# A dense-GELU layer's forward and backward: from the scheduler's order with packed tails to a fixed emission order with metered derivative work

## The chip, the cores and the metric

One core of a Trainium2 chip runs one program. The metric is the device time of one execution in microseconds (us). All times are medians of several executions unless one look is named. The experiments ran in three rounds, each on one chip; the kernel before took 320.8 to 321.4 us (medians) on all three, so runs of different rounds are compared directly. Unless a text says otherwise, runs are of the fast state (within 1.5% of the fastest run of the same kernel). "Span" is the time from the first to the last instruction of the one execution that was profiled; a run's time is 1.7 to 2.2 us above its span here.

Engine names in the profile: PE is TensorE's matmuls, PEld its weight loads, DVE is VectorE, ACT is ScalarE, POOL is GpSimd, SP issues most DMA. A trailing q (SPq, POOLq) is the engine's instruction queue.

## The reference

```python
# x: [1, 2048, 448], w1: [448, 1792], w2: [1792, 448], all bf16
h   = gelu_tanh(x @ w1 + b1)
out = h @ w2 + b2
# returned: out and the gradients of x, w1, b1, w2, b2 for a given grad_out
```

The gradient of x needs `gelu'(z)` with `z = x @ w1 + b1`. Both kernels compute it elementwise (E below), store it in place of z as `Z`, and use it in the backward: `gh = (Z + 1) * (grad_out @ w2^T)`.

## The kernel before

The program has four stages, each limited by TensorE at best:

1. Forward, 4 blocks of 512 rows x 7 pairs of 128 hidden columns = 28 steps. A step is a pair of z tiles (`pair_mms`) and the second product of the step before (`chain_step`).
2. grad_w2: 14 sums of 16 matmuls.
3. Backward: 28 steps like the forward's, with w2^T and w1^T.
4. grad_w1: 6 + 2 x 1 sums of the same kind.

The contraction of 448 is 3 x 128 + 64. The kernel before packs the 64-row tails of the two tiles of a pair into the two halves of the array:

```python
def pair_mms(pss, lhs, rhs, fts):
    for h, ft in enumerate(fts):                       # 3 full matmuls for each tile
        for n, kt in enumerate((0, 1, 3) if h == 0 else (0, 1, 2)):
            nc.tensor.matmul(pss[h], lhsT=lhs[:, kt, fc], rhs=rhs[:, kt, :], start=(n == 0), stop=False)
    for h, ft in enumerate(fts):                       # the two 64-row tails, side by side
        kt, ps_ = (2, slice(0, DL)) if h == 0 else (3, slice(DL, P))
        nc.tensor.matmul(pss[h], lhsT=lhs[ps_, kt, fc], rhs=rhs[ps_, kt, :], start=False, stop=True)
```

The derivative of one pair is three ScalarE and seven VectorE operations on 128x1024 tiles. The letters are used throughout:

```python
def emit_E(b, c):
    nc.scalar.activation(out=s, in_=zc, func=ACT.Square)             # ScalarE
    nc.vector.tensor_scalar(out=v, in0=s, ...)                       # u, first half
    nc.vector.tensor_tensor(out=v, in0=v, in1=zc, op=ALU.mult)       # u, second half
    nc.scalar.activation(out=v, in_=v, func=ACT.Tanh, scale=GELU_C)  # ScalarE
    nc.scalar.activation(out=n, in_=v, func=ACT.Square)              # ScalarE
    nc.vector.tensor_scalar(out=y, in0=s, ...)
    nc.vector.tensor_tensor(out=y, in0=y, in1=zc, op=ALU.mult)
    nc.vector.tensor_scalar(out=n, in0=n, scalar1=-1.0, scalar2=1.0, ...)
    nc.vector.tensor_tensor(out=y, in0=y, in1=n, op=ALU.mult)
    nc.vector.tensor_tensor(out=zc, in0=y, in1=v, op=ALU.add)        # Z is final
```

No order is laid down: a scheduler orders each engine's instructions, with the forward's matmuls and evictions marked as high priority. x block 0 is transposed on TensorE with an identity matrix, b1 too, and b1 is added in ScalarE's evictions (four of 128x512 a step: gelu and identity for two tiles).

## Time and profile before

| | before |
|---|---|
| time | 321.35 us (321.01 to 321.94, 3 runs; 321.19 with the fourth that came with the result) |
| span of the profiled run | 318.7 us |
| first useful matmul | 20.9 us |
| forward, 28 steps | 20.9 to 127.5 us, 3.8 us a step |
| grad_w2 | 127.5 to 170.1 us |
| start of the backward, with its stall | 170.1 to 183.7 us |
| backward at a steady step | 3.24 us a step |

The table of windows of the kernel before, cut near the stage borders (the second row ends with the first 1.7 us of the backward's matmuls, from 170.1). After the window and its length it gives busy us and, in brackets, instructions of each engine, then the granted TensorE clock, the DMA share and GB/s.

```profile
core 0: us, PE busy (x) PEld busy (x) DVE busy (x) ACT busy (x) POOL busy (x), PEclk, DMA share, GB/s
20.90:127.50 106.60, 101.23 (x448) 38.97 (x449) 56.03 (x107) 102.71 (x152) 5.93 (x5) 0.99 0.51 105
127.50:171.80 44.30, 44.30 (x235) 22.63 (x234) 43.47 (x86) 42.88 (x52) 7.04 (x8) 1.00 0.59 122
171.80:183.70 11.90, 4.39 (x18) 1.32 (x16) 11.83 (x27) 8.46 (x9) 0.71 (x1) 0.73 0.69 186
183.70:271.50 87.80, 87.77 (x425) 37.17 (x426) 37.34 (x115) 6.13 (x14) 2.29 (x3) 0.98 0.52 109
...
```

In the forward ScalarE is the full engine (102.7 of 106.6 us). In the third row VectorE is full (11.83 of 11.9) and TensorE does 4.4 us of work: the backward wants `Z`, and VectorE still owes derivatives. The clock of 0.73 there is the price of the pause: after the longest wait, of 4.8 us, four matmuls take 1.67 us (at 183.73), where four at 176.30 take 0.93.

The start, from the timeline of the kernel before (start, duration, engine, line, operation, and in brackets what the engine waited for):

```profile
12.87 0.28 POOL masks.py:199 TENSOR_SCALAR_AFFINE_SELECT ident<-ident 128x128 bf16<-128x128 bf16 x1 [10.27 <-issue]
12.99 0.64 DVE L220 TENSOR_TENSOR gsum<-g_all 128x448 f32<-128x448 bf16 x1 [11.86 <-DMA g_all<-in_grad_out_dram]
...
13.66 5.89 DVE L222 TENSOR_TENSOR gsum<-gsum,g_all 128x448 f32<-128x448 f32 x9
...
19.47 0.41 DVE L127 COPY xT_q<-acc 128x512 bf16<-128x512 bf16 x1
...
20.90 1.01 PE L71 MATMUL ps<-xT_q,w_sb 128*128 128x512 bf16 x2 [0.79 <-DVE b1c L132]
```

The scheduler hoisted the sums for grad_b2 (gsum) ahead of the copy of the transposed x, so VectorE first waited for g_all and then added for 6 us.

VectorE on derivative work, from the timeline of VectorE alone, kernel before:

```profile
143.32 0.42 DVE L152 TENSOR_SCALAR y<-s 128x1024 bf16<-128x1024 bf16 x1
143.65 0.42 DVE L154 TENSOR_SCALAR n<-n 128x1024 bf16<-128x1024 bf16 x1
143.99 0.68 DVE L149 TENSOR_TENSOR v<-v,Z_100 128x1024 bf16<-128x1024 bf16 x1
144.59 0.69 DVE L155 TENSOR_TENSOR y<-y,n 128x1024 bf16<-128x1024 bf16 x1
```

The starts are 0.33 to 0.34 us apart behind a TENSOR_SCALAR and 0.60 behind a TENSOR_TENSOR.

### The profile page before, as it was taken

To read this page: it belongs to the slowest core of one execution; us is meant where nothing else is said; L and a number is where in the kernel's file an instruction comes from. 1 tells how busy PE (TensorE), PEld (TensorE's weight loads), DVE (VectorE), ACT (ScalarE), POOL (GpSimd) and SP (SyncE) were. 2 spreads that over 40 slices of the span, in tenths; PEclk is the share of its full clock that TensorE was granted. 3 is DMA by queue.
4 is the path that set the end of the run, shared out by engine and by line. 5 is a ranking of instruction groups with operands and counts; after the bars stand their busy time and mean duration, and the time that the engine had idled before them with its cause. 6 is when DMAs were issued, how large, how long until landed. Compare 5 with 4: busy or idle time off the path is not lost.

```text
span 318.7 us, 3910 instructions
## 1 busy us (share of the span) xinstructions
PE 288.4 (91%) x1408; PEld 125.9 (40%) x1408; DVE 156.8 (49%) x348; ACT 171.5 (54%) x244; POOL 19.3 (6%) x26
## 2 busy tenths in 40 slices
PE   7238999999999997999997399999999999999994
PEld 2213343333333333555553034444444444555552
DVE  0380438267466558999999964343534343000000
ACT  1117999999999999999999600200200200312211
POOL 2003000100000000111002000000000000100000
PEclk9659999999999999999999679999999999999999
DMA  7993436735633556997004743665754554210111
GB/s 218 355 228 61 70 80 134 145 68 116 156 67 81 108 132 139 203 220 168 29 29 125 181 82 69 151 121 100 180 93 99 123 100 82 89 45 29 43 45 29
DMA packets 97998, 36.62 MB, mean 115 GB/s; under 512 B 90044, under 2 KB 95532, under 8 KB 97980
## 3 DMA queue, kind: packets, MB, share of 16 engines
q1 hardware_dynamic: 94924, 27.17, 41.3%
q0 software_dynamic: 2512, 8.95, 9.1%
q10 hardware_dynamic: 544, 0.26, 0.3%
q8 instruction: 11, 0.18, 0.2%
q14 instruction: 7, 0.06, 0.1%
HBM read 7.69 MB, written 6.89 MB: 46 GB/s over the span
## 4 chain that ended last, share of the span: by engine, by line
PE 63%; DVE 22%; ACT 9%; DMA 4%; issue 2%; DVEq 0%; POOL 0%; POOLq 0%; ACTq 0%
PE acc L138 23%; PE ps L71 20%; PE acc L276 11%; PE ps L75 6%; DMA g_all<-in_grad_out_dram 4%; DVE y L155 3%; DVE v L149 3%; DVE y L153 3%; ACT hT L180 3%; DVE v L148 2%; PE acc L284 2%; DVE gsum L222 2%; DVE n L154 2%; DVE y L152 2%; ACT Z_101 L181 1%
## 5 line engine op out<-in xcount | busy, mean ns | idle before, releaser
L138 PEld LDWEIGHTS <-hT 128*128 128x128 bf16 x448 | 38.7, 98 | 59.8 <-issue 14.1
L138 PE MATMUL acc<-w_sb,hT 128*128 128x448 bf16 x224 | 55.1, 354 | 3.5 <-ACT hT L180 2.4
L138 PE MATMUL acc<-w1T_sb,hT 128*128 128x448 bf16 x224 | 47.6, 358 | 7.5 <-DVE hT L242 7.5
L164 ACT ACTIVATE o_blk<-acc 128x448 bf16<-128x448 f32 x16 | 7.4, 550 | 82.3 <-issue 41.7
L71 PE MATMUL ps<-xT_q,w_sb 128*128 128x512 bf16 x168 | 45.9, 388 | 2.6 <-DVE b1c L132 0.8
L212 PE MATMUL acc<-g_all,h_nat 128*128 128x448 bf16 x224 | 42.5, 352 | 0.0
L71 PE MATMUL ps<-gT_q,w2T_sb 128*128 128x512 bf16 x168 | 42.2, 387 | 0.0
L180 ACT ACTIVATE hT<-ps,b1c 128x512 bf16<-128x512 f32 x56 | 38.5, 734 | 3.9 <-PE ps L75 3.7
L276 PE MATMUL acc<-gh_nat,x_all 128*128 128x448 bf16 x192 | 36.7, 352 | 0.0
L150 ACT ACTIVATE v<-v 128x1024 bf16<-128x1024 bf16 x28 | 30.0, 1086 | 3.2 <-DVE v L149 3.2
L151 ACT ACTIVATE n<-v 128x1024 bf16<-128x1024 bf16 x28 | 30.2, 1091 | 0.2
L212 PEld LDWEIGHTS <-h_nat 128*128 128x128 bf16 x224 | 21.9, 98 | 20.5
L71 PEld LDWEIGHTS <-w_sb 128*128 128x128 bf16 x168 | 16.4, 99 | 28.8 <-issue 13.7
L276 PEld LDWEIGHTS <-x_all 128*128 128x128 bf16 x192 | 18.6, 98 | 17.6 <-issue 0.4
L154 DVE TENSOR_SCALAR n<-n 128x1024 bf16<-128x1024 bf16 x28 | 11.8, 421 | 26.1 <-ACT n L151 26.1
L71 PEld LDWEIGHTS <-w2T_sb 128*128 128x128 bf16 x168 | 16.3, 99 | 18.9 <-issue 1.8
L278 ACT ACTIVATE gw_t<-acc 128x448 bf16<-128x448 f32 x12 | 6.5, 543 | 29.3 <-PE acc L276 27.3
L148 DVE TENSOR_SCALAR v<-s 128x1024 bf16<-128x1024 bf16 x28 | 11.9, 425 | 15.3 <-ACT s L147 14.3
L155 DVE TENSOR_TENSOR y<-y,n 128x1024 bf16<-128x1024 bf16 x28 | 19.2, 687 | 0.3
L75 PE MATMUL ps<-xT_q,w_sb 64*128 64x512 bf16 x56 | 17.5, 384 | 0.0
L165 POOL DMA_DIRECT2D out_dram<-o_blk x8 | 6.2, 770 | 172.2 <-DVE o_blk L162 99.1
L242 DVE SCALAR_TENSOR_TENSOR hT<-Z_99,ps 128x512 bf16<-128x512 bf16 x14 | 9.1, 686 | 13.5 <-PE ps L75 13.5
(69 smaller groups left out, 256.7 us busy)
## 6 DMA issues: line engine op xcount, KB each, us to landing
out_dram<-o_blk POOLq DMA_DIRECT2D x8, 448.0 KB, 4.0
g_all<-in_grad_out_dram POOLq DMA_DIRECT2D x1, 1792.0 KB, 11.7
x_all<-in_x_dram POOLq DMA_DIRECT2D x1, 1792.0 KB, 9.2
out_dram<-gw_t POOLq DMA_DIRECT2D x7, 224.0 KB, 3.0
out_dram<-gw_t SPq DMA_DIRECT2D x12, 112.0 KB, 1.7
w_sb<-in_w_dram SPq DMA_DIRECT2D x1, 1120.0 KB, 12.3
h_nat<-hT SPq DMA_TRANSPOSE x56, 2.4
gh_nat<-hT SPq DMA_TRANSPOSE x56, 2.5
```

Of the source, the lines that this page charges most:

```text
L71: nc.tensor.matmul(pss[h], lhsT=lhs[:, kt, fc], rhs=rhs[:, kt, :], start=(n == 0), stop=False)
L75: nc.tensor.matmul(pss[h], lhsT=lhs[ps_, kt, fc], rhs=rhs[ps_, kt, :], start=False, stop=True)
L138: nc.tensor.matmul(acc[j][:, 0:D], lhsT=lhs[:, h, j * P:(j + 1) * P], rhs=w[:, ft, :], start=(ft == 0), stop=(ft == NF - 1))
L148: nc.vector.tensor_scalar(out=v[:], in0=s[:], scalar1=GELU_A, scalar2=1.0, op0=ALU.mult, op1=ALU.add)
L149: nc.vector.tensor_tensor(out=v[:], in0=v[:], in1=zc, op=ALU.mult)
L150: nc.scalar.activation(out=v[:], in_=v[:], func=ACT.Tanh, scale=GELU_C)
L151: nc.scalar.activation(out=n[:], in_=v[:], func=ACT.Square)
L154: nc.vector.tensor_scalar(out=n[:], in0=n[:], scalar1=-1.0, scalar2=1.0, op0=ALU.mult, op1=ALU.add)
L155: nc.vector.tensor_tensor(out=y[:], in0=y[:], in1=n[:], op=ALU.mult)
L180: nc.scalar.activation(out=hT[:, h, :], in_=pss[h][:], func=ACT.Gelu_apprx_tanh, bias=b1c[:, ft:ft + 1])
L212: nc.tensor.matmul(ps_w[:, 0:D], lhsT=h_nat[:, st, ft * P:(ft + 1) * P], rhs=g_all[:, st, :], start=(st == 0), stop=(st == NS - 1))
L276: nc.tensor.matmul(ps_w[:, 0:CW], lhsT=x_all[:, st, kt * P:(kt + 1) * P], rhs=gh_nat[:, st, cs], start=(st == 0), stop=(st == NS - 1))
```

## The change: intent and diff

The intent is a plan in which TensorE never waits: one fixed order on all engines, the pipeline laid out by hand, and the derivative, which is off the critical path, dealt out in small portions ("metered") where an engine is thought to be idle. The diff, cut to its core:

```diff
+    ctx.enter_context(tc.manual_schedule())          # every engine in emission order
-    psum_z ... bufs=4 tiles of 128x512
+    psum_z ... bufs=2 tiles of 128x2x512             # one eviction of 128x1024 for a pair
+    class Background:                                # queues "V" (VectorE) and "A" (ScalarE)
+        def step(self, dve, act):                    # adds credits; emits queued operations
+            for e, c in (("V", dve), ("A", act)):    # while credit > 0 and their
+                self.credit[e] = min(self.credit[e] + c, 4.0)   # predecessor is emitted
+            ...
 # pair_mms: packed tails -> a fourth full matmul; rows 0..63 of its weights are zero,
 # but row 0 holds b1 and row 0 of xT holds ones
+            for kt in range(KD):
+                nc.tensor.matmul(ps[:, h, :], lhsT=lhs[:, kt, ...], rhs=rhs[:, kt, :], ...)
+    xq = load_x(0)                                   # x block 0 by DMA transpose, no identity
 # forward, step p
+            nc.scalar.activation(out=hT[:], in_=ps[:], func=ACT.Gelu_apprx_tanh)
+            nc.scalar.activation(out=Z[b][:, 2 * c:2 * c + 2, :], in_=ps[:], func=ACT.Identity)
+            if pc % 2 == 0:                          # 16 of 28 pairs now; uses hT, one Square less
+                emit_E(pb, pc, hist[p - 1], p - 1, prevs, False)
+            else:
+                late.append((pb, pc))                # 12 "late" pairs, in grad_w2
+        bg.step(dve, STEP - 2.16)                    # STEP = 3.24
 # zero rows of w2T for the padded backward
+    nc.gpsimd.memset(w2T_sb[0:DL, KD - 1, :], 0.0)
+    for k, (b, c) in enumerate(late):
+        emit_E(b, c, None, 100 + k, prevs, True)
+    for st in range(1, NS): bg.add("V", 0.65, lambda st=st: gsum_op(st), ("gsum", st))
 # grad_w2, after each of 14 evictions
+            bg.step(3.03, 3.03 - 0.55)
 # backward, step p
+            bg.need(("E", b, c))
+        bg.step(STEP - 1.4, STEP - 0.5)
... (weight loads in smaller pieces, shorter warm-up, identity built late)
```

For a late pair, ScalarE's order becomes Square(k), Tanh(k), Square(k), then Square(k+1); VectorE's is u(k), y(k), then the last three operations of pair k-1.

## The prediction

> **What bounds the kernel now.** TensorE is the longest engine (288 of 318.7 us busy), yet the trace splits into stages with different limits (timeline and the table of windows):
> - Start, 0 to 20.9 us: the first useful matmul begins at 20.9. The identity came at 12.9; two VectorE copies of the transposed x wait behind the bias-gradient sums (gsum, hoisted to 13 us) until 19.5 and 20.3; b1's transpose and cast follow.
> - Forward, 20.9 to 127.5: ScalarE is busy in every window (8.0 of 8 us). It evicts four 128x512 tiles a step (one every 0.57 us) and runs three 128x1024 derivative operations (one every 0.95). A step takes about 3.8 us;
> - grad_w2, 127.5 to about 171.5: TensorE at full rate, 0.19 us a matmul. VectorE works off the derivative.
> - Backward, to 271.5: TensorE waits for VectorE (chain of waits: 7.5 us at the hT of line 242, single waits of 2.7 and 4.8), works at half rate from 176 to 187, then runs at exactly 3.24 us a step.
> - grad_w1 42.9 us, end 4.3 us: unchanged.
>
> **What the change does.**
> 1. x block 0 comes by DMA transpose (such transfers land in 2.7 to 3.6 us) with nothing of gsum, identity or b1 before it. First useful matmul at about 7.5 us: minus 13 us.
> 2. Forward: ScalarE's evictions become two 128x1024 operations, about 0.95 us each like those of that width now, plus one Tanh on 16 of 28 steps: 68 us in all, against about 90 of TensorE. Even pairs cost VectorE about 4.0 us each (starts 0.60 and 0.34 us apart), 64 us plus 10 for output rows. Both fit; TensorE binds.
> 3. The padded tail: a packed pair of 64-row tails takes 0.32 us between full matmuls, of which 0.1 us lies on each side of the mode switch (tails at 193.44, chain at 193.76). Two full matmuls take 0.43. So 3.23 a step before, 8x0.216+1.52=3.25 after: a wash. The Trainium skill, "TensorEngine Tiling (Array Packing)", Key Properties, says that changing the tiling mode drains the array; this trace agrees with about 0.1 us at each switch.
> 4. Late derivatives (12 pairs, about 3.5 us VectorE and 2.9 us ScalarE each) and gsum (9.8 us) are metered into grad_w2's 42.6 us; a few us spill into the backward, where VectorE has 1.8 us spare a step. The stall at its start goes: minus 12 us.
>
> Sum: 7.5 start + 1.7 cold clock + 90.7 forward (28x3.24) + 2 stalls + 42.6 + 90.7 backward + 2 stalls + 42.9 + 4.3 = 284.4 us of span; the run's time is 2 to 2.6 above the span: **287 us**, range 281 to 294. Cold clock: the first matmuls at 20.9 are 0.43 us apart, as the Trainium skill, "TensorE: Matmul & The Clock Gate", Part 1, says of an idle array.
>
> Chances: faster by over 2% 0.97, within 2% 0.025, slower by over 2% 0.005.
>
> **What would show each step.** First xT matmul near 7.5 us; the forward at 3.24 us a step with ScalarE below 85% and TensorE bound; the step in backward still 3.24; no half-clock slice between grad_w2 and backward.
>
> **What would make it wrong.** In-order ScalarE and VectorE queues blocking each other (Tanh waiting for u, evictions behind it) would lift the forward step; transposes of hT queued behind the weight loads in SP's queue; or the x transposes contending with the weights and landing after 9 us. A derivative backlog early in backward would cost 3 to 8 us.

## The result, and the profile after

| | before | after | predicted |
|---|---|---|---|
| time | 321.19 us (4 runs) | 296.79 us (295.08 to 297.68, 4 runs) | 287, 281 to 294 |
| span | 318.7 | 295.5 | 284.4 |
| first useful matmul | 20.9 | 5.57 | 7.5 |
| end of forward | 127.5 | 104.1 | 101.9 |
| grad_w2 | 42.6 | 43.9 | 42.6 |
| backward, stall and cold clock with it | 101.4 | 100.4 | 92.7 |

The ratio of after to before is 0.923 (0.918 to 0.928). Ratios are the mean time of one kernel's fast runs over that of the other's in the same rounds, so not quite the ratio of the medians quoted. "Backward" counts from the first of its matmuls, 170.1 in the kernel before and about 148.0 after.

The direction was right, but the gain was 24 us and not 34. Against the predicted span the stages give: start -1.9, forward +4.1, grad_w2 +1.3, backward +7.7, the rest -0.1, together +11.1 us, which is the whole of 295.5 - 284.4. Against the kernel before, the backward, which was to lose 12 us of stall, lost 1.0, and grad_w2 grew by 1.3.

The same table of windows, kernel after:

```profile
5.57:104.00 98.43, 93.89 (x449) 43.89 (x449) 74.60 (x131) 69.38 (x72) 5.79 (x8) 1.00 0.74 153
104.00:148.00 44.00, 42.69 (x226) 21.90 (x225) 37.08 (x67) 30.44 (x36) 5.85 (x7) 1.00 0.65 131
148.00:158.80 10.80, 3.58 (x18) 1.44 (x17) 9.71 (x20) 8.77 (x12) 1.43 (x2) 0.89 0.06 21
158.80:248.30 89.50, 89.50 (x433) 42.87 (x434) 53.27 (x144) 10.96 (x20) 6.92 (x6) 0.97 0.67 136
...
```

ScalarE is no longer the forward's limit (69 of 98 us). But the third row is still there: 10.8 us with 3.6 us of TensorE work. The pause at the start of the backward, which the prediction had going away, is still there, only earlier. Note also the second row: in grad_w2 VectorE is busy 37 of 44 us and ScalarE 30, so neither engine is full by its busy time, and yet they fall behind.

What TensorE waited for, kernel after (total us, times, longest; the wait for the warm-up operand and one of 0.7 us for the first x are left out):

```profile
PE acc L170 <- DVE hT L337: 7.2, 1, 7.2
PE acc L170 <- ACT hT L257: 4.5, 6, 1.2
PE acc L318 <- ACT gw_t L320: 1.3, 2, 1.1
...
```

The start, kernel after, from the timeline: SP issues the x transpose at once and TensorE begins at 5.57.

```profile
0.76 1.38 SPq L207 DMA_TRANSPOSE xT_q<-in_x_dram  x1
...
5.57 5.66 PE L163 MATMUL ps<-xT_q,w_sb 128*128 128x512 bf16 x16 [0.72 <-DMA xT_q<-in_x_dram]
```

The forward's waits come at block borders. From the timeline of all engines at the second border:

```profile
55.65 2.22 DVE L232 TENSOR_TENSOR o_blk<-acc,b_bc 128x448 bf16<-128x448 f32 x4 [3.04 <-PE acc L170]
...
59.18 0.69 DVE L118 TENSOR_TENSOR v<-v,Z_103 128x1024 bf16<-128x1024 bf16 x1
...
59.96 1.06 ACT L121 ACTIVATE v<-v 128x1024 bf16<-128x1024 bf16 x1 [2.75 <-DVE v L118]
...
60.93 1.00 ACT L257 ACTIVATE hT<-ps 128x1024 bf16<-128x1024 f32 x1
...
61.99 1.69 PE L170 MATMUL acc<-w_sb,hT 128*128 128x448 bf16 x8 [0.27 <-ACT hT L257]
```

Read it upwards: TensorE waits for the gelu eviction (L257); that stands behind a Tanh (L121) in ScalarE's queue; the Tanh waited 2.75 us for u (L118); and u stood behind the four output rows (L232), which had waited for TensorE. The Trainium skill, "TensorE: Matmul & The Clock Gate", under "Architectural detail", says that the queues of ScalarE and VectorE are strict FIFO, first in, first out; the trace agrees: the eviction at 60.93, whose matmuls had ended at about 58.5, stood some 2.4 us behind a Tanh that nobody needed yet and that itself waited 2.75 us. The next step of the same border waits 1.2 us more for L257 (66.63 us), behind the next Tanh.

VectorE on one late pair, kernel after (timeline of VectorE alone):

```profile
139.69 0.43 DVE L117 TENSOR_SCALAR v<-s 128x1024 bf16<-128x1024 bf16 x1 [0.31 <-ACT s L111]
140.16 0.69 DVE L118 TENSOR_TENSOR v<-v,Z_104 128x1024 bf16<-128x1024 bf16 x1
140.76 0.42 DVE L126 TENSOR_SCALAR y<-s 128x1024 bf16<-128x1024 bf16 x1
141.22 0.69 DVE L127 TENSOR_TENSOR y<-y,Z_104 128x1024 bf16<-128x1024 bf16 x1
141.83 0.42 DVE L136 TENSOR_SCALAR n<-n 128x1024 bf16<-128x1024 bf16 x1
142.28 0.69 DVE L140 TENSOR_TENSOR y<-y,n 128x1024 bf16<-128x1024 bf16 x1
143.01 0.69 DVE L141 TENSOR_TENSOR Z_103<-y,v 128x1024 bf16<-128x1024 bf16 x1
```

The next pair begins at 144.01, so a pair takes 4.31 us. Now four of the seven operations read what the one before them just wrote, and the gaps are 0.46 behind a TENSOR_SCALAR and 0.73 behind a TENSOR_TENSOR in that case. There is also a wait of 0.31 us for ScalarE's Square.

Last, a wait of ScalarE in the middle of grad_w2, first POOL's side and then ScalarE's (timelines of one engine each, kernel after):

```profile
117.28 1.59 POOL L283 MEMSET w2T_sb<- 64x1792 bf16 x1 [11.04 <-DMA w2T_sb<-in_w_dram]
118.82 0.71 POOL L322 DMA_DIRECT2D out_dram<-gw_t  x1
```

```profile
127.51 0.53 ACT L320 CAST gw_t<-acc 128x448 bf16<-128x448 f32 x1 [3.91 <-DMA out_dram<-gw_t]
```

The zeroing of w2T's padding waits in POOL's queue for w2T to land. The stores of grad_w2 stand behind it, the eviction needs one of two buffers back, and ScalarE stands for 3.9 us with the late derivatives behind it. Part of the wait is the store's own landing: issued at 118.82, it frees the buffer only at 127.5, while w1^T is being transposed by DMA (issued at 117.64, landing after 11.4 us). Without the zeroing (e7) the first store is issued at 115.05, before that transpose, and nothing waits.

So there were four candidates for the 11 us: the period of a late pair, the store wait, the order in which the first backward product queues behind late pairs (11 of them by count of VectorE's instructions), and the border waits. The rival for the first three was plain capacity: that VectorE's work does not fit.

### The profile page after: what moved, and what is told of

Its sections match the earlier page's. It is cut to its first block, busy times and chain, and to the rows that moved or that the text cites. A ratio compares the mean times of both kernels' runs of the same rounds, so it can differ in the third digit from the quotient of the medians.

```text
span 295.5 us, 3804 instructions
## 1 busy us (share of the span) xinstructions
PE 276.4 (94%) x1396; PEld 133.3 (45%) x1396; DVE 175.9 (60%) x362; ACT 128.1 (43%) x153; POOL 22.0 (7%) x31
## 4 chain that ended last, share of the span: by engine, by line
PE 69%; ACT 9%; DVE 9%; DMA 8%; issue 3%; SPq 1%; POOL 1%; ACTq 0%; POOLq 0%; DVEq 0%
PE ps L163 27%; PE acc L170 25%; PE acc L378 12%; DMA out_dram<-gw_t 3%; ACT v L121 3%; DVE v L118 2%; ACT s L111 2%; DVE o_blk L232 2%; PE acc L388 2%; PE acc L318 2%; DVE v L117 2%; ACT hT L257 2%; DMA h_nat<-hT 2%; DMA xT_q<-in_x_dram 2%; DMA w2T_sb<-in_w_dram 2%
## 5 line engine op out<-in xcount | busy, mean ns | idle before, releaser
L170 PEld LDWEIGHTS <-hT 128*128 128x128 bf16 x448 | 43.6, 99 | 58.1 <-DVE hT L337 7.7
L163 PE MATMUL ps<-xT_q,w_sb 128*128 128x512 bf16 x224 | 54.8, 390 | 0.7 <-DMA xT_q<-in_x_dram 0.7
L163 PE MATMUL ps<-gT_q,w2T_sb 128*128 128x512 bf16 x224 | 53.6, 383 | 0.0
L170 PE MATMUL acc<-w_sb,hT 128*128 128x448 bf16 x224 | 46.8, 353 | 4.5 <-ACT hT L257 4.5
L121 ACT ACTIVATE v<-v 128x1024 bf16<-128x1024 bf16 x28 | 29.6, 1058 | 32.1 <-DVE v L118 32.1
L163 PEld LDWEIGHTS <-w_sb 128*128 128x128 bf16 x224 | 22.4, 100 | 27.5 <-issue 3.6
L257 ACT ACTIVATE hT<-ps 128x1024 bf16<-128x1024 f32 x28 | 28.5, 1018 | 13.9 <-PE ps L163 13.7
L163 PEld LDWEIGHTS <-w2T_sb 128*128 128x128 bf16 x224 | 22.2, 99 | 25.9 <-issue 1.5
L337 DVE SCALAR_TENSOR_TENSOR hT<-Z_104,ps 128x512 bf16<-128x512 bf16 x14 | 9.1, 685 | 13.6 <-PE ps L163 13.6
L337 DVE SCALAR_TENSOR_TENSOR hT<-Z_105,ps 128x512 bf16<-128x512 bf16 x14 | 9.1, 685 | 13.5 <-PE ps L163 13.5
L232 DVE TENSOR_TENSOR o_blk<-acc,b_bc 128x448 bf16<-128x448 f32 x16 | 8.9, 617 | 10.7 <-PE acc L170 10.7
L131 ACT ACTIVATE n<-v 128x1024 bf16<-128x1024 bf16 x12 | 12.7, 1057 | 0.4
```

What stands on the lines that cost most here:

```text
L121: nc.scalar.activation(out=t["v"][:], in_=t["v"][:], func=ACT.Tanh, scale=GELU_C)
L131: nc.scalar.activation(out=n[:], in_=t["v"][:], func=ACT.Square)
L163: nc.tensor.matmul(ps[:, h, :], lhsT=lhs[:, kt, ft * P:(ft + 1) * P], rhs=rhs[:, kt, :], start=(kt == 0), stop=(kt == KD - 1))
L170: nc.tensor.matmul(acc[j][:, 0:D], lhsT=lhs[:, h, j * P:(j + 1) * P], rhs=w[:, ft, :], start=(ft == 0), stop=(ft == NF - 1))
L232: nc.vector.tensor_tensor(out=blk[:, j, :], in0=acc[j][:, 0:D], in1=b2_bc[:], op=ALU.add)
L257: nc.scalar.activation(out=hT[:], in_=ps[:], func=ACT.Gelu_apprx_tanh)
```

## The experiments

Twelve kernels ran; all gave correct results. Each is the changed kernel with the edit shown, unless said otherwise.

### e1_late_s_ahead: the next Square ahead of Tanh, for late pairs

```diff
         bg.add("A", 1.09, s_, ("s", k), ...)          # Square of this pair
+        while pend:                                    # then what the pair before left behind
+            bg.add("A", *pend.pop(0))
-        bg.add("A", 1.09, tanh_, ("t", k), ("u", k))   # late pairs only:
-        bg.add("A", 1.09, sq_, ("q", k))
+        pend.append((1.09, tanh_, ("t", k), ("u", k)))
+        pend.append((1.09, sq_, ("q", k)))
```

> Only the order on ScalarE of the late derivative pairs is changed: the Square of pair k+1 is issued ahead of Tanh and Square of pair k; the VectorE order is identical to the changed kernel. Theory A (lock step: Square, then u on VectorE, then Tanh and Square on ScalarE, then the next Square, 4.31 us a pair, with the first backward product queued behind 11 such pairs): the period falls to 3.5 to 3.7 us, the 7.2 us stall at the start of the backward falls to 0 to 3 us, span 287 to 291. Rival B (VectorE is simply full, its work does not fit): period and stall stay, span 294 to 296.

Measured: 293.58 us (291.47 to 295.21), profiled span 289.7 (the fastest of the four). The stall was 4.0 us instead of 7.2. The period fell only from 4.31 to 4.11 us: once the Squares were early, VectorE ran without a pause, and still took 4.11 us for operations that I had sized at 3.5. So the lock step between the engines was 0.2 us of the period, and most of my miss lay within VectorE's own queue. Neither theory came out as written: the period is VectorE's, as the rival said, but the stall did shrink. From the timeline of VectorE in e1, the start of a pair, its last operation, and the start of the next:

```profile
139.66 0.43 DVE L118 TENSOR_SCALAR v<-s 128x1024 bf16<-128x1024 bf16 x1
142.97 0.69 DVE L142 TENSOR_TENSOR Z<-y,v 128x1024 bf16<-128x1024 bf16 x1
143.77 0.43 DVE L118 TENSOR_SCALAR v<-s 128x1024 bf16<-128x1024 bf16 x1
```

The last gap is 0.80 us, though u does not read Z. But v has two buffers, so u writes the buffer that the operation before it has just read. Where the mixing begins, the same two neighbours are 0.61 us apart in e6, where v has three buffers (113.27 to 113.88), and 0.80 in e10, where it has two (113.74 to 114.54). So a pair is 3.42 us for independent neighbours (3 x 0.34 + 4 x 0.60), 0.49 for four dependent ones and 0.20 for the buffer used again: 4.11.

### e2_gw2_bufs4: four buffers for grad_w2's output

```diff
-        gw2_t = tmp.tile([P, 2, D], BF16, name="gw2_t")
+        gw2_t = tmp.tile([P, 2, D], BF16, name="gw2_t", bufs=4)
```

> Only the buffers of the grad_w2 output tile go from 2 to 4. Theory: ScalarE's 3.9 us wait at 123.6 us for a grad_w2 store (held back by the zeroing of w2T's tail in POOL's queue and by the w1 transpose on the DMA engines) goes away, TensorE's 1.1 and 0.2 us waits in grad_w2 shrink, and the backward stall falls from 7.2 to 3 to 4 us; span 290 to 292. Rival: the wait is slack that the 4.31 us lock step would have used up anyway (the first product still at about 158 us): span unchanged within 1 us.

Measured: 296.64 us (294.74 to 297.61). In the profile the store wait and TensorE's waits in grad_w2 are gone, but the period stays 4.31 and the stall is 5.9 us; the profiled run, with a span of 292.7, was the fastest of four. The median is that of the kernel after, so by time this edit alone is not resolved. The wait is real; what it is worth is seen only together with a shorter period, in e10.

### e3_tanh_later: the forward's Tanh one derivative pair later

```diff
+        while pend:                                    # at the next derivative pair
+            bg.add("A", *pend.pop(0))
-        bg.add("A", 1.09, tanh_, ("t", k), ("u", k))   # the forward's pairs only:
+        pend.append((1.09, tanh_, ("t", k), ("u", k)))
```

> Only the Tanh of the forward's derivative pairs is issued later on ScalarE (after the evictions of the following step or steps). Theory: at each of three block borders Tanh waits for u on VectorE, which stands behind the output rows, and the evictions behind Tanh come late: 0.3 and 1.2 us of TensorE wait per border, 4.5 us in all. These waits go; the forward ends at 98 to 100 us instead of 104, but since the lock step of the late pairs begins no earlier than VectorE's backlog allows, the span falls by 3 to 5 us, to 290.5 to 292.5. Rival: the border waits are VectorE's backlog itself (accumulators come free late) and reappear on another line: span falls by less than 1.5 us.

Measured: 293.12 us median (293.04 to 297.09), profiled span 291.1. All six border waits are gone, and grad_w2 begins at 97.97 us. That is 5.5 + 1.7 + 28 x 3.24, within 0.1 us: the forward with no wait at all. But of the 6.1 us only some 4 arrived. From TensorE's waits in e3:

```profile
PE acc L176 <- DVE hT L345: 9.9, 1, 9.9
```

The stall at the backward grew from 7.2 to 9.9 us: TensorE came to the backward 7.4 us earlier (140.57 instead of 147.92), VectorE to the first product only 4.7 us earlier (153.31 instead of 158.01). A gain in one stage was partly taken back by the next one's limit.

### e4_fewer_in_gw2: less late work in front of the backward

```diff
-            bg.step(3.03, 3.03 - 0.55)
+            bg.step(2.2, 2.2 - 0.4)
```

> Only the metering in grad_w2 is changed: 2.2 and 1.8 credits per tile instead of 3.03 and 2.48, which puts 8 instead of 11 late pairs in front of the first backward product on VectorE; the same work in total. Theory A (order, not capacity): the product is ready about 13 us earlier than TensorE needs it, so the 7.2 us stall and the cold clock after it (about 2.3 us) go, backward steps stay 3.24 us: span 285 to 288. Rival B (VectorE's capacity): the work moved into the backward stalls its steps instead; span 292 to 296.

Measured: 287.85 us, three fast runs of 287.17 to 287.89 (spans 285.4 to 285.9), ratio 0.897. The same work in the same two engines, with 8 late pairs in front of the first product instead of 11, and TensorE's waits for VectorE at the start of the backward fell to 0.7 us:

```profile
PE acc L170 <- DVE hT L337: 0.7, 1, 0.7
```

The later backward steps stayed at 3.24 us, but for one of 3.66 (both in the profiled run, in which ScalarE's store wait was even 8.7 us and the period of a late pair still 4.31). Capacity over the whole kernel is therefore not the limit; the order in one queue is. One constant was worth about 9 us.

The profiled run of e4 was its slow one (292.40), and it shows another thing. From its TensorE timeline:

```profile
12.34 1.25 PE L163 MATMUL ps<-xT_q,w_sb 128*128 128x512 bf16 x5 [2.14 <-DMA w_sb<-in_w_dram]
13.43 3.04 PE L170 MATMUL acc<-w_sb,hT 128*128 128x448 bf16 x8
```

TensorE waited 2.1 us for a piece of w1 and then worked at half rate (eight matmuls in 3.04 us instead of 1.68) until about 17. The profiled runs of e1 and e6 have such a wait for w1 as well (1.4 and 1.3 us), those of e2, e3 and e7 have none. In e1 and e6 the wait cost nothing, for the matmuls around it ran faster than in the kernel after: the first chain_step began at 10.95 and 11.05 us, against 11.07 there and 13.43 in e4. It appears to be a matter of the run (no edit above touches the loads), and it has to be looked for before two spans are compared.

### e5_combined: e1, e2, e3 and e4 together

> The four edits so far together: Square ahead for the late pairs, Tanh later in the forward, four grad_w2 output buffers, lower metering in grad_w2. If each removes its own wait: no TensorE wait in the forward (saves 6 us), none in grad_w2 (1.3 us), none at the start of the backward (7.2 us and the cold clock after it); span 279 to 283 where the start does not wait for w1, about 4 us more where it does; time 281 to 285 in fast runs. If the forward's 6 us only come back as backlog later: 285 to 288, as with the lower metering alone.

Measured: 282.64 us (280.58 to 283.48), ratio 0.878 (0.874 to 0.883), profiled span 278.8. Once its first pairs are through (1.4 us of waits for w1 there), TensorE's list of waits has nothing more until the end. The gain over the kernel after, 14.2 us, is somewhat less than the sum of the four edits' own gains (3.2 + 0.2 + 3.7 + 8.9 = 16.0 us); e1, e2 and e4 all work on the same stall.

### e6_interleave: VectorE's operations of two late pairs mixed

```diff
-  VectorE: v<-s(k) v*z(k) y<-s(k) y*z(k) n(k-1) y*n(k-1) Z(k-1)
+  VectorE: v<-s(k) n(k-1) v*z(k) y*n(k-1) y<-s(k) Z(k-1) y*z(k)      # on top of e1; v has 3 buffers
```

> Square ahead (as e1) and in addition the seven VectorE operations of a late pair k interleaved with the last three of pair k-1, so that no operation reads what the one just before it wrote; a third buffer for v. Nothing else changes, and as many late pairs stand in front of the first backward product as in e1. Theory C (a VectorE operation that depends on the one just before it starts about 0.12 us later, 0.46 instead of 0.34 and 0.72 instead of 0.60, which made the period 4.11 us in e1): the period falls to 3.4 to 3.7 us, the first product comes at 147 to 150 us instead of 153, and the 4.0 us stall of e1 falls to under 1 us; span 285 to 288 where the start does not wait for w1. Rival D (VectorE's 4.11 us is a fixed cost, or a conflict with ScalarE for the same memory): the period stays at 4.0 us or more, and the stall at 3 us or more.

Measured: 291.94 us median (289.63 to 292.97 in three fast runs, one slow of 299.06). The period fell to between 3.4 and 3.8 us. From the timeline of VectorE in e6:

```profile
143.10 0.69 DVE L174 TENSOR_TENSOR y<-y,n 128x1024 bf16<-128x1024 bf16 x1
143.70 0.42 DVE L178 TENSOR_SCALAR y<-s 128x1024 bf16<-128x1024 bf16 x1
144.03 0.68 DVE L179 TENSOR_TENSOR Z<-y,v 128x1024 bf16<-128x1024 bf16 x1
144.64 0.69 DVE L180 TENSOR_TENSOR y<-y,Z 128x1024 bf16<-128x1024 bf16 x1
```

The same operations, of the same length, start 0.33 and 0.60 us apart, as in the kernel before. So theory C holds: a VectorE operation that needs the result of the one just before it starts about 0.12 us later: some 0.04 us after the other's end, where an independent one starts about 0.09 us before it. The mixed order also keeps u away from the operation that last read its buffer of v. The prediction for the stall missed, though: it was 3.9 us, because ScalarE now stood 6.8 us at the grad_w2 store instead of 3.5.

### e7_packed_bwd: the padding undone in the backward

```diff
-    nc.gpsimd.memset(w2T_sb[0:DL, KD - 1, :], 0.0)
-            pair_mms(ps, w2T_sb, gq, fts)
+            pair_mms_packed(ps, w2T_sb, gq, fts)      # 6 full matmuls, 2 packed tails, as before
```

> The padded tail is undone in the backward alone (two packed 64-row tails, no zeroing of w2T's tail). The prediction's claim is a wash: backward step 3.23 to 3.25 us, as with the padding; 28 steps, so under 0.5 us in all. If the padding was worth the mode switches: 3.3 to 3.4 us a step, up to 4 us more. The zeroing also leaves POOL's queue, so the 3.9 us ScalarE wait for a grad_w2 store should shrink or go; as in e2 that alone gives at most 1 to 3 us.

Measured: 294.46 us (293.64 to 294.93). From TensorE's timeline in e7, one backward step and the start of the next:

```profile
176.84 1.69 PE L180 MATMUL acc<-w1T_sb,hT 128*128 128x448 bf16 x8
178.36 1.46 PE L170 MATMUL ps<-gT_q,w2T_sb 128*128 128x512 bf16 x6
179.75 0.39 PE L174 MATMUL ps<-gT_q,w2T_sb 64*128 64x512 bf16 x2
180.08 1.69 PE L180 MATMUL acc<-w1T_sb,hT 128*128 128x448 bf16 x8
```

The step is 180.08 - 176.84 = 3.24 us, and the padded one is 3.24 us too (chains at 164.25 and 167.49 in the kernel after). The padding is a wash, as predicted: a fourth matmul costs what two changes of the tiling mode cost. The store wait went with the zeroing, and the stall fell to 5.8 us, as in e2.

### e8_no_manual and e11_no_manual_again: the emission order undone

```diff
-    ctx.enter_context(tc.manual_schedule())
```

> The changed kernel with the emission order undone: one line less, so the scheduler orders every engine again, as in the kernel before; padding, ones row, wide evictions, transposed x block and split derivative stay. If the emission order is what pays: the scheduler moves ready work (gsum, late derivatives) forward, the step of the forward rises above 3.24 us and the time is 305 to 325. If the other parts pay: within 2% of the changed kernel, 291 to 303.

> e8 again, timed: the changed kernel without the line for emission order. e8's single run was 292.06 against 296.79, although its start lost some 8 us (first full run of matmuls at 13.9 us, behind g_all hoisted to 1.3 us). If that was no accident: 290 to 294 in fast runs, so emission order as such loses 1 to 2% here, and forward at 3.24 us a step without ScalarE waits. If it was: 295 to 299.

Measured: 292.06 us (one look, state unknown) and then 292.87 us (291.23 to 293.71), ratio 0.912 (0.907 to 0.916) against 0.923 (0.918 to 0.928) for the kernel after. With everything else of the change in place, the scheduler beats the fixed order, by about 1%; the intervals do not meet. It has no ScalarE waits in the forward, and a stall of 2.7 and 3.5 us instead of 7.2. It loses at the start. From the timeline of e11:

```profile
1.30 1.33 POOL L262 DMA_DIRECT2D g_all<-in_grad_out_dram  x1 [0.86 <-POOLq L408]
...
13.14 1.44 PE L162 MATMUL ps<-xT_q,w_sb 128*128 128x512 bf16 x3 [3.09 <-POOL xT_q L212]
```

It hoists the load of g_all to 1.3 us, and the ones row of x, which POOL writes after that, comes at 12.6. The first chain_step begins at 16.69 us (17.78 in e8) instead of 11.07, so 5.6 and 6.7 us are lost there. The fixed order loads g_all at 23.7 us, and its ones row came at 5.8.

### b1_manual_only: the emission order alone, on the kernel before

```diff
     tmp = ctx.enter_context(tc.tile_pool(name="tmp", bufs=2))
+    ctx.enter_context(tc.manual_schedule())            # on the kernel before
```

> The kernel before with the line for emission order added and nothing else. In that order ScalarE does per step four evictions (2.3 us), Square, Tanh, Square (2.85 us) and waits for VectorE's v between them (about 1.2 us): 6.3 to 6.7 us a step instead of 3.8; then grad_w2 finds no derivative left over and the backward no stall. Forward about 180 us, total 365 to 385. If emission order itself pays: under 321 us.

Measured: 414.17 us (one look, state unknown). From ScalarE's timeline:

```profile
78.22 0.67 ACT L181 ACTIVATE hT<-ps,b1c 128x512 bf16<-128x512 f32 x1
...
82.78 1.06 ACT L151 ACTIVATE v<-v 128x1024 bf16<-128x1024 bf16 x1 [1.22 <-DVE v L150]
...
84.84 0.67 ACT L181 ACTIVATE hT<-ps,b1c 128x512 bf16<-128x512 f32 x1
```

A step takes 84.84 - 78.22 = 6.62 us, near the 6.3 to 6.7 expected. The total is higher than I expected because TensorE also waits 34 us for g_all, which is loaded only when its line is reached. The same one-line switch costs about 1% with the new plan and 29% without it.

### e10_inter_bufs4: e6 and four buffers

> e6 (Square ahead, VectorE interleaved) plus four grad_w2 output buffers; v back to two buffers for room; metering as in the changed kernel, 11 late pairs in front of the first backward product. In e6 the period fell to about 3.5 us but ScalarE stood 6.8 us at a grad_w2 store, and the stall stayed 3.9 us. If period and store wait are the whole stall: no store wait, first product before 149 us, stall under 0.7 us, span 286 to 289. If something else holds the first product: stall still 2 us or more.

Measured: 286.59 us (286.37 to 288.39), ratio 0.895. v is back at two buffers, as the expectation says. The period is 3.4 to 3.8 us (one of 4.9 apart), ScalarE does not wait for a store, the first product starts at 149.30 us, and TensorE does not wait at the start of the backward at all, with all 11 late pairs still in front of it. Period and store wait are the whole stall; e4 removes it without touching either, by order. TensorE's one large wait that is left is the border's:

```profile
PE acc L202 <- ACT hT L289: 4.5, 6, 1.2
```

### e9_w1_before_b1: e5 with one load moved

```diff
-    nc.scalar.dma_start(out=w1_sb[0:1, KD - 1, :], in_=b1...)
     load_w1(nc.scalar, 256, 512)
+    nc.scalar.dma_start(out=w1_sb[0:1, KD - 1, :], in_=b1...)
```

> The combined kernel (e5) with one line moved: on ScalarE's DMA queue the second piece of w1 is issued before the b1 row. In e5 TensorE waited 1.4 us for w1 in the profiled run, and e4's slow run waited 2.1 us with the half clock going on after it. If the late second piece is what spreads the runs of e5 (280.6 to 283.5): no w1 wait, runs within 1 us, 280 to 281.5 median. If the b1 row was what mattered more (its landing now later): the wait moves to the first tail matmul, 282 to 284.

Measured: 281.66 us, four runs within 281.36 to 281.86, ratio 0.877 (0.8745 to 0.8801). The wait for w1 is gone and the runs lie within 0.5 us of each other. A wait of 1.2 us for the ones row took its place, so the best start of e5 (280.58) was not beaten. The median is not resolved from e5's (ratio 0.878, 0.874 to 0.883). e9 is 12.3% under the kernel before and about 5% under the change as it was made.

## Why the prediction was right or wrong, point by point

**Start: right, and better than said.** 5.57 us instead of 7.5. One part of it was off the other way: the x transpose landed 4.8 us after its issue, not 2.7 to 3.6, so the better number is owed to the margin that the 7.5 held. e8 and e11 show that the DMA transpose and the ones row alone do not do it: with g_all hoisted the third run of matmuls begins at 13.1 to 13.9 us.

**Forward's step: right in its steady part, undersized at the borders.** The step is 3.24 us and ScalarE is at 70%. I allowed 2 us of waits and 6.1 were lost, of which 4.5 are listed as waits. The mechanism I named as what could go wrong (Tanh waiting for u, evictions behind it) is the one; e3 took it away and the forward came to its sum within 0.1 us. What I did not see is where: VectorE's output rows must wait for TensorE at a block's end, and two even pairs (6 and 0) follow each other there.

**Padding: right.** 3.24 us with and without it (e7). The Trainium skill, "TensorEngine Tiling (Array Packing)", Key Properties, has the mode switch drain the array; the trace shows about 0.1 us on either side.

**The step that failed: "Late derivatives (12 pairs, about 3.5 us VectorE and 2.9 us ScalarE each) ... are metered into grad_w2's 42.6 us; a few us spill into the backward ... The stall at its start goes: minus 12 us".** The stall was 7.2 us, and with the cold clock behind it the backward took 7.7 us more than I allowed. The term that was mis-sized is the period of a late pair. I read 0.34 and 0.60 us from a stretch of trace in which neighbours did not depend on each other and used them for an order in which they do: 4.11 us within VectorE (e1: 0.49 for dependent neighbours, 0.20 for the buffer of v), plus 0.2 of waiting for ScalarE, makes 4.31. From the first late pair's u to the eleventh's, 110.16 to 156.94 us, ten periods took 46.8 us instead of 35.0: about 8 us more by the period, and 3.4 by the store wait, which I had not foreseen. By this estimate, at 3.5 us a pair the product would have been ready at 147.0, 4.6 us before TensorE could use it at 151.5; so 7.2 of the 11.8 us came out as the stall. Some 2.3 us of half clock followed (in the two groups of eight matmuls behind the stall), and my allowance was 2. The prediction did name the risk, a backlog early in the backward that "would cost 3 to 8 us", but left it out of its sum. The second error was to think of credits as time: metering decides only the order, and an in-order VectorE put 11 of the late pairs before the first backward product, however late they ran. That VectorE had 1.8 us to spare in each backward step was true (e4 used it) and of no help where the order didn't allow it.

**grad_w2: +1.3 us,** TensorE's waits for evictions behind the same store wait; they are gone in e2.

**Cold clock: right.** The first matmuls are 0.43 us apart. The Trainium skill, "TensorE: Matmul & The Clock Gate", Part 1, gives 426.7 ns for 512 columns on a cold array, which this trace agrees with.

**Credit given to the emission order.** The prediction did not say how much of the gain was the order's. By e11 it is negative here (about 1%), by b1 it is a disaster without the plan. What paid, by e11, were the other parts together: wide evictions, split derivative, early start, padding; no run takes the first three apart. With its constants right the fixed order (e5, e9) is some 10 us under e11, but the scheduler was not run with e5's buffers, so what the order itself is worth there is not shown.

**Left open.** Why e2's timed runs do not follow its profile, and why e7, with the same stall, is 2.2 us faster than e2, is not settled. Nor is it shown whether POOL in e11 was held by the g_all load itself or by x transposes landing late beside it.

## What to carry to other kernels

In a hand-made order, size off-path work from a stretch with the same neighbours: an operation starts 0.34 us after a TENSOR_SCALAR of this size that it does not depend on and 0.46 us after one whose result it reads, one that overwrites a buffer just read pays too (0.80 instead of 0.60 behind a TENSOR_TENSOR), and mixing two work items brings the shorter gaps back. Metering by estimated cost only sets an order, so leave slack before the first instruction that the critical engine needs from that queue, and keep everything that may wait (a Tanh, a memset behind a DMA) behind it. When a stage's stall is removed, look at the next stage before counting the gain: 6 us saved in the forward gave 4, until the backward's stall was gone as well.

## What the Trainium skill lacked or had wrong

- "VectorE: DVE Perf Modes", "The DRAIN you can't avoid", says that a next operation that is not held starts before the pipe is empty, and here that is so: an independent operation starts 0.33 to 0.34 us after a 128x1024 TENSOR_SCALAR of 0.42 us and 0.60 us after a TENSOR_TENSOR of 0.69 us. What the page lacks is the price of a dependence on the operation just before: 0.46 and 0.73 us, and 0.80 for overwriting the buffer that a TENSOR_TENSOR has just read. Over a pair of seven operations that is 3.42 against 4.11 us, so with the count of operations the same the order alone is worth 0.69 us a pair.
- "TensorEngine Tiling (Array Packing)", Key Properties, states the drain of a mode switch but not its size: about 0.1 us on each side of a packed pair of 512 columns, which here makes packing two 64-row tails worth nothing against one more full matmul for each tile (3.24 us a step either way).
- The pages cited here say that the queues are strict FIFO, not what follows when several of them meet (no page has this number): a POOL memset that waits for a DMA held stores, and through two buffers stopped ScalarE for 3.9 us (6.8 in e6, 8.7 in e4's profiled run).
